# Top-32 attention, FFN and mixture of experts on one core: second-layer weights in the key and value buffers, and a third transpose buffer

## The chip, the core and the metric

The kernel runs on one core of one Trainium2 chip. The metric is the device time of one execution in microseconds (us), lower is better. A step below is one turn of the kernel's planned loop.

## What is computed

```python
# q, k, v: 4 batches x 8 heads x 576 x 64
scores = scale * np.matmul(q, k.transpose(0, 1, 3, 2))
kth = np.partition(scores, -32, axis=-1)[..., -32:-31]
scores = np.where(scores >= kth, scores, -1e9)
attn = softmax(scores)                       # written out in the reference
x = (attn @ v).transpose(0, 2, 1, 3).reshape(2304, 512)
h = np.maximum(np.maximum(x @ w1, x @ w2), x @ w3)      # 512 -> 768
x = h @ w_out                                           # 768 -> 512
logits = x @ w_gate                                     # 8 experts
expert_idx = np.argmax(logits, axis=1)
gate_w = softmax(logits)[arange, expert_idx]
for e in range(8):                                      # each token, one expert
    ye = np.maximum(x[mask_e] @ w1[e], 0.0) @ w2[e]     # 512 -> 1024 -> 512
    out[mask_e] = gate_w[mask_e, None] * ye
```

## The kernel before, in words

Every fp32 operand is kept as a sum of two fp16 parts, hi and lo, and a product is three matmuls (hi hi, hi lo, lo hi). A weight piece is split where it is loaded: ScalarE writes the hi part, scales the fp32 piece into a PSUM tile, and VectorE subtracts (`split_piece`, `lo_part`, lines L734 and L735).

**The loop of steps.** The 4 x 8 heads of 576 queries are 144 tiles of 128 queries. A Python loop plans the whole program: at step t it starts tile t (scores on TensorE, ScalarE's copy of them `s` at L890, VectorE's scan in chunks at L904) and issues for older tiles the later stages, each at a fixed lag: the candidates' rounds, threshold, k-th value, exponential (`st_exp`, L1031), mask, the probabilities' hi part `phl` (L1042, ScalarE), their lo part (L1046, GpSimd), a transposing DMA on SP's queue from `phl` to `pt` (`st_ptr`, L1051), and two steps later the matmuls of `pt` with the values (`av`, L1065). Tiles with n % 4 above 1 ("early") take the exponential in the step of the split's predecessor, `t - L_MASK`; the others at `t - L_EXP`, one step earlier, and their mask follows as VectorE's bulk work at `t - L_MASK`. There are three `phl` tiles and two `pt` buffers; TensorE must have read a `pt` before SP may issue the next transposition into it, and what SP's queue holds behind waits with it.

**Work between.** Each step also has credits with which `run_units` issues units of other work: the FFN's jobs (18 blocks of 128 tokens; six units of 36 matmuls of 128 columns at L356, two with WO, the gate, and a ranking that counts tokens per expert, L1224 and L1225), and, from the middle on, slots of the fullest expert. A slot is 128 tokens of that expert, gathered as soon as enough are ranked. Early slots run the first layer in two halves in the attention, with weights W1h, one half of the columns at a time: `half_piece` loads its four pieces of 128 x 512 in four steps through one staging tile `he` (L1300 is the split's ScalarE copy; there are three such loads, the last at steps 124 to 127); results go to a DRAM buffer `hs`. Their second layer (`unit_e2`, four units of six matmuls of 512 columns, L367 to L369) needs W2e. In the kernel before, W2e is a tile of a pool `e1` that opens at step 145, and its eight pieces load at steps 146 to 153. Each slot's `hTe` is read back from `hs` on SP's queue (L1356), two at a time.

**The end.** The last tile's av is at step 157. From there TensorE has FFN jobs, second layers, and late slots; when all blocks are ranked, `finale` goes through the other experts' tiles in the order of a table that VectorE makes from the ranking's counts (its last operation is at L332), the first of them with a transposing load (L428) on SP.

**Memory.** Keys (`kT`) and values (`vh`, `vl`) of a batch have two buffers each, taken in turn by batches 0 to 3. `hsel` keeps nine selection values per query of every group of four tiles. Ahead of step 0 the K and Q pieces are split into tiles of the pools `e` (four) and `f` (two) (`split_tile`).

The lines of the planner that set the credits and the weights' time:

```python
credit[0] = min(credit[0] + (TAIL_RATE if e2 else EARLY_RATE if slots else UNIT_RATE), 2.5 if e2 else CAP)
elif e1 and len(eld) < (KE + 2 * KD if e2 else KE):
    after(2, piece(len(eld)))
```

## Time and profile before

| | us |
|---|---|
| median of 3 runs | 979.85 |
| lowest and highest | 979.28, 984.86 |
| the profiled execution | 983.39 |
| its span | 981.7 |
| last av ends | 758.06 |
| last ranking matmul starts | 818.53 |

Busy shares of the span: TensorE (PE) 77%, VectorE (DVE) 77%, ScalarE (ACT) 71%, GpSimd (POOL) 62%. These are means over an attention in which all of them work and a tail in which TensorE does nearly alone. A row of the stretches gives, for a stretch from A to B, its length and each engine's busy time and number of instructions; PEld is TensorE's weight load. A row of waits names the waiting instruction, the engine and line that ended the wait, and the sums. In a timeline, brackets behind a row tell how long the engine was idle before it, and for what. SPq and ACTq are the queues' own times for issuing a DMA, not the transfers.

### The profile page before, as it was taken

What the parts mean: (1) busy time and instruction counts of PE and PEld (TensorE: products, weight loads), DVE (VectorE), ACT (ScalarE), POOL (GpSimd) and SP (SyncE); (2) the same over time, 40 slices, a digit from 0 to 9 for tenths busy, and PEclk for the clock granted to TensorE, in tenths of its full rate; (3) what the DMA queues carried; (4) which work ended last, traced back from release to release, by engine and by line L of the source; (5) the groups of instructions that cost most, each with busy time, mean ns of one, the idle gap of its engine ahead of it and who ended that gap; (6) DMA issues with size and microseconds to landing.
All of it is one profiled execution on the core that took longest, in us unless ns stands there. A gap on an engine that the chain in (4) does not pass through costs nothing. (4 is left out here: it accounts for less than half of the span.)

```text
span 981.7 us, 28988 instructions
## 1 busy us (share of the span) xinstructions
PE 754.9 (77%) x10606; PEld 581.5 (59%) x10606; DVE 757.6 (77%) x3109; ACT 695.2 (71%) x1462; POOL 605.9 (62%) x553
## 2 busy tenths in 40 slices
PE   0212358888887898968798896889887999999992
PEld 0100237667556586856677675677765775678781
DVE  4999999998897998978987996898934335457671
ACT  2678899998888788988978787688663231456661
POOL 1457798999696789968766888588862221111110
PEclk9999979999998999999899899899999999999997
DMA  9672987868987887999978786588668477799270
GB/s 254 177 240 58 210 154 133 139 128 126 194 151 163 127 159 139 188 172 151 181 129 135 142 143 144 107 138 142 129 137 175 127 207 263 187 295 230 56 208 16
DMA packets 372164, 155.93 MB, mean 159 GB/s; under 512 B 331931, under 2 KB 348319, under 8 KB 372000
## 3 DMA queue, kind: packets, MB, share of 16 engines
q1 hardware_dynamic: 368128, 143.10, 72.8%
q0 software_dynamic: 3136, 9.46, 3.0%
q8 instruction: 87, 1.43, 0.6%
q10 hardware_dynamic: 736, 1.32, 0.5%
q14 instruction: 77, 0.63, 0.3%
HBM read 76.06 MB, written 16.67 MB: 94 GB/s over the span
## 5 line engine op out<-in xcount | busy, mean ns | idle before, releaser
L356 PEld LDWEIGHTS <-W 128*128 128x128 f16 x4560 | 252.6, 101 | 28.3 <-issue 23.0
L956 POOL TENSOR_TENSOR f<-s,g 128x576 f32<-128x576 f32 x144 | 192.6, 1337 | 75.3 <-ACT g L950 29.0
L356 PE MATMUL mm<-xT,W 128*128 128x128 f16 x3456 | 218.4, 226 | 22.3 <-DVE W1h L735 11.7
L883 PE MATMUL S<-kT,qT 128*128 128x512 f16 (+3 forms) x640 | 109.7, 316 | 132.7 <-ACT s L890 116.3
L1046 POOL TENSOR_TENSOR phl<-e,phl 128x576 f16<-128x576 f32 x144 | 188.2, 1307 | 24.4 <-ACT phl L1042 22.1
L904 DVE MAX8 c<-s 128x8 f32<-128x96 f32 x864 | 174.7, 242 | 19.1 <-ACT s L890 18.7
L883 PEld LDWEIGHTS <-qT 128*128 128x128 f16 (+1 forms) x640 | 55.6, 107 | 192.8 <-issue 160.4
L1065 PE MATMUL av<-vh,pt 128*128 128x65 f16 (+3 forms) x1600 | 110.6, 200 | 37.1 <-DMA pt<-phl 22.1
L1042 ACT ACTIVATE phl<-e 128x576 f16<-128x576 f32 x144 | 97.6, 678 | 38.2 <-DMA pt<-phl 38.0
L1065 PEld LDWEIGHTS <-pt 128*128 128x128 f16 (+3 forms) x2400 | 88.4, 102 | 51.8 <-DMA pt<-phl 24.7
L1031 ACT ACTIVATE e<-s,be 128x576 f32<-128x576 f32 x144 | 110.4, 767 | 4.9 <-POOL s L1025 3.2
L965 DVE MAX8 vec<-f 128x8 f32<-128x576 f32 x144 | 108.8, 756 | 3.8 <-POOL f L956 1.0
L950 ACT ACTIVATE g<-s,bf 128x576 uint16<-128x576 f32 x144 | 111.0, 771 | 0.1
L890 ACT ACTIVATE s<-S 128x576 f32<-128x576 f32 x144 | 92.1, 640 | 12.8 <-PE S L883 12.0
L1036 DVE SCALAR_TENSOR_TENSOR e<-s,kth,e 128x576 f32<-128x576 f32 x72 | 100.0, 1389 | 0.0
L1065 PE MATMUL av<-vl,pt 128*128 128x64 f16 (+3 forms) x800 | 100.0, 197 | 0.0
L457 DVE SCALAR_TENSOR_TENSOR W<-st,W 128x1024 f16<-128x1024 f32 x56 | 65.8, 1221 | 38.3 <-ACT W L456 33.2
L1025 POOL TENSOR_TENSOR s<-s,g 128x576 f32<-128x576 f32 x72 | 95.2, 1322 | 0.3
L1149 POOL TENSOR_TENSOR hhl<-a,hhl 128x384 f16<-128x384 f32 x36 | 36.6, 1016 | 33.4 <-ACT hhl L1148 33.4
L356 PE MATMUL mm<-xTe,W1h 128*128 128x128 f16 x768 | 51.0, 229 | 7.5 <-DMA xTe<-xs 5.7
L456 ACT ACTIVATE W<-st 128x1024 f16<-128x1024 f32 x56 | 55.5, 1047 | 0.0
L1022 ACT ACTIVATE g<-s,kth 128x576 uint16<-128x576 f32 x72 | 55.3, 768 | 0.0
(222 smaller groups left out, 1533.1 us busy)
## 6 DMA issues: line engine op xcount, KB each, us to landing
st<-in_moe_w_dram SPq DMA_DIRECT2D x72, 512.0 KB
raw<-in_moe_w_dram SPq DMA_DIRECT2D x12, 512.0 KB
st<-in_v_dram SPq DMA_DIRECT2D x16, 256.0 KB
hs<-he SPq DMA_DIRECT2D x16, 256.0 KB
st<-in_moe_w_dram SPq DMA_DIRECT2D x16, 256.0 KB
hTe<-hs SPq DMA_DIRECT2D x8, 512.0 KB
st<-in_q_dram SPq DMA_DIRECT2D x15, 256.0 KB
qT<-qT SPq DMA_DIRECT2D x30, 128.0 KB
```

What stands on the lines that cost most here:

```text
L356: nc.tensor.matmul(out=ps[:, o * n:(o + 1) * n], lhsT=w(b, kk, c), rhs=x(a, kk), start=(kk == 0 and i == 0), stop=(kk == KD - 1 and i == 2))
L883: nc.tensor.matmul(out=ps[o:o + m, j, 0:(REM if j else NQ * P)], lhsT=qt[:, vv, hh, 0:m], rhs=kr[:, hh] if j else km[:, hh // HG, :, hh % HG],
L904: nc.vector.max(out=c[:, i * 8:(i + 1) * 8], in_=s[:, i * CW:(i + 1) * CW])
L950: nc.scalar.activation(out=gg[n], in_=Ss[n], func=ACTF.Sign, bias=bf[g][:, i], accum_out=cnt[g][:, i])
L956: nc.gpsimd.tensor_tensor(out=ff[n], in0=Ss[n], in1=gg.pop(n).bitcast(F16), op=ALU.subtract)
L965: bulk.append(lambda: nc.vector.max(out=y8[g][:, i, 1:9], in_=y))
L1025: nc.gpsimd.tensor_tensor(out=Ss[n], in0=Ss[n], in1=zz.pop(n).bitcast(F16), op=ALU.subtract)
L1031: nc.scalar.activation(out=e, in_=Ss.pop(n) if early(n) else Ss[n], func=ACTF.Exp, scale=ESC, bias=be[g][:, i])
L1036: nc.vector.scalar_tensor_tensor(out=e, in0=Ss.pop(n), scalar=kth[g][:, i:i + 1], in1=e, op0=ALU.is_ge, op1=ALU.mult)
L1042: nc.scalar.activation(out=ph[:, 0, 0:S], in_=p, func=ACTF.Copy)
L1046: nc.gpsimd.tensor_tensor(out=ph[:, 1, 0:S], in0=p, in1=ph[:, 0, 0:S], op=ALU.subtract)
L1065: nc.tensor.matmul(out=av[o:o + m, i, 0:n], lhsT=t[0:kk, p * NCH + c, o:o + m], rhs=v_rows(x, b, c, hh)[:, 0:n], start=(c == 0 and p == 0 ...
```

## The change

Keys and values of the even batches get a pool of their own, `kvl`, with one tile each (`kt0`, `vh0`, `vl0`), which batch 2 is the last to use; the odd batches have the pools of before with one buffer. When batch 2's scores are through (from step 109, pieces 0 to 3 into `kt0`) and its av are through (from step 124, pieces 4 to 7 into `vh0` and `vl0`), the W2e pieces are written there, through the three staging tiles `st` that K, Q and V used. With all eight loaded, the early slots' second layers are issued in the attention, one slot at a time until `e1` opens and two after that, and the credits of a step grow by 1.8 (`LATE_RATE`) instead of 1.4. `half_piece` uses the same staging, and its third load comes at steps 128 to 131 instead of 124 to 127. `pt` gets a third buffer. To pay for the memory: the exponential of the other half of the tiles goes to the step of its mask, with three `e` tiles instead of four (`NE3`, also in `split_tile`); `hsel` keeps two groups, and the verdict counts the k-th values above zero (`hkth`) instead of `hsel`'s ones; small tiles have fewer buffers. The gate's weights load at step 0 instead of 5, and the values' column of ones isn't written again for batch 2.

```diff
-    NSWAP, XLAG, KLAG, TSTOP, EARLY_RATE = 4, 2, 2, 140, 1.4
+    NSWAP, XLAG, KLAG, TSTOP, EARLY_RATE, LATE_RATE = 4, 2, 2, 140, 1.4, 1.8
...
+        NE3 = L_LO - L_MASK + 1
...
+            kvl = p1.enter_context(tc.tile_pool(name="kvl", bufs=1))
+            kt0 = kvl.tile([P, H * S], F16, name="kt0")
+            vh0 = kvl.tile([P, NCH, H, D + 1], F16, name="vh0")
+            vl0 = kvl.tile([P, NCH, H, D], F16, name="vl0")
...
-            kv_p = p_at.enter_context(tc.tile_pool(name="kv", bufs=2))
+            kv_p = p_at.enter_context(tc.tile_pool(name="kv", bufs=1))
...
-            k_p = p_op.enter_context(tc.tile_pool(name="kp", bufs=2))
+            k_p = p_op.enter_context(tc.tile_pool(name="kp", bufs=1))
...
-                hsel = a_p.tile([P, NG, G, 9], F16, name="hsel")
+                hsel = a_p.tile([P, NHS, G, 9], F16, name="hsel")
+                hkth = a_p.tile([P, NG, G], F32, name="hkth")
...
-                    tag = ("e", L_LO - L_EXP + 1) if lead_n[0] < L_LO - L_EXP + 1 else ("f", NFB)
+                    tag = ("e", NE3) if lead_n[0] < NE3 else ("f", NFB)
...
-                    kt = k_p.tile([P, H * S], F16, tag="kT", name="kT")
+                    kt = k_p.tile([P, H * S], F16, tag="kT", name="kT") if b % 2 else kt0
...
-                e = wk_p.tile([P, S], F32, tag="e", name="e", bufs=L_LO - L_EXP + 1)
+                e = wk_p.tile([P, S], F32, tag="e", name="e", bufs=NE3)
...
-                t = wk_p.tile([P, 2 * NCH, P], F16, tag="pt", name="pt", bufs=L_AV - L_PTR)
+                t = wk_p.tile([P, 2 * NCH, P], F16, tag="pt", name="pt", bufs=L_AV - L_PTR + 1)
...
+            FREE = 3 * (NTL // B)
+
+            def w2e(e, kk):
+
+                if kk < KE // 2:
+                    return kt0[:, (e * (KE // 2) + kk) * DM:(e * (KE // 2) + kk + 1) * DM]
+                y = (vh0, vl0)[e].rearrange("p t h d -> p (t h d)")
+                return y[:, (kk - KE // 2) * DM:(kk - KE // 2 + 1) * DM]
+
+            def stage():
+                return e1[0].tile([P, DM], F32, tag="st", name="st", bufs=3) if e1 else stage_tile()
+
+            def piece_ok(i):
+
+                if i >= KE:
+                    return bool(e2) and i < KE + 2 * KD
+                return bool(picked) and clock[0] > picked + 8 and clock[0] > FREE + (0 if i < KE // 2 else L_AV + 1)
...
-                st = ew[0].tile([P, DM], F32, tag="he", name="he")
+                st = stage()
...
-                            if sum(o.hT is not None and not o.late and o.u < 8 for o in slots) < 2:
-                                s.hT = e1[0].tile([P, 2 * KE, P], F16, tag="hTe", name="hTe", bufs=2)
+                            if sum(o.hT is not None and not o.late and o.u < 8 for o in slots) < (2 if e1 else 1):
+                                s.hT = (e1 or ew)[0].tile([P, 2 * KE, P], F16, tag="hTe", name="hTe",
+                                                          bufs=2 if e1 else 1)
...
-                credit[0] = min(credit[0] + (TAIL_RATE if e2 else EARLY_RATE if slots else UNIT_RATE), 2.5 if e2 else CAP)
+                credit[0] = min(credit[0] + (TAIL_RATE if e2 else LATE_RATE if len(eld) >= KE else EARLY_RATE if slots
+                                             else UNIT_RATE), 2.5 if e2 else CAP)
...
-                    n = t - L_EXP
+                    n = t - L_MASK
                     if ok(n) and not early(n):
                         st_exp(n)
...
-                    elif e1 and len(eld) < (KE + 2 * KD if e2 else KE):
-                        after(2, piece(len(eld)))
+                    elif piece_ok(len(eld)):
+                        (after(2, piece(len(eld))) if e1 else pend_w.append(piece(len(eld))))
                         eld.append(t)
```

The order of ScalarE shows the pieces and the exponential. Here are about two steps of before, around step 125: L890 is the score copy of a new tile, L950 and L1022 are older tiles' selections, L1042 writes `phl`, L1300 and L734 split a piece of W1h.

```order
L1022 ACTIVATE g<-s,kth 128x576
L1042 ACTIVATE phl_143<-e 128x576
L1300 ACTIVATE W1h<-he 128x512
L734 ACTIVATE mm<-he 128x512
L940 ACTIVATE bf<-T_12353 128x1
L890 ACTIVATE s<-S 128x576
L950 ACTIVATE g,cnt<-s,bf 128x576
L1022 ACTIVATE g<-s,kth 128x576
L1042 ACTIVATE phl_144<-e 128x576
L1300 ACTIVATE W1h<-he 128x512
L734 ACTIVATE mm<-he 128x512
```

The same two steps after the change (the lines are some 10 to 30 higher; L1328 is the ScalarE copy of a piece, L1043 the exponential):

```order
L1034 ACTIVATE g<-s,hkth 128x576
L1054 ACTIVATE phl_149<-e 128x576
L1328 ACTIVATE vh_108<-st 128x512
L740 ACTIVATE mm<-st 128x512
L1043 ACTIVATE e<-s,be 128x576
L949 ACTIVATE bf<-T_12381 128x1
L899 ACTIVATE s<-S 128x576
L959 ACTIVATE g,cnt<-s,bf 128x576
L1034 ACTIVATE g<-s,hkth 128x576
L1054 ACTIVATE phl_150<-e 128x576
L1328 ACTIVATE vh_108<-st 128x512
L740 ACTIVATE mm<-st 128x512
```

Where a piece of W1h was split, one of W2e is now, into `vh0`; W1h's pieces follow four steps later. An exponential stands between the piece and the next score copy.

The order of SP ahead of the finale's first tile, before (L449 loads weights of the next expert, L1356 the last slot's `hTe`, L428 the first tile's rows):

```order
L449 ISA
L449 DMA st_15743<-in_moe_w_dram 128x2x512
L449 ISA
L449 DMA st_15743<-in_moe_w_dram 128x2x512
L1356 DMA hTe<-hs 128x2048
L422 TENSOR_LOAD roi
L422 ISA x2
L428 ISA
L428 DMA_TRANSPOSE W1h<-xs 128x8x128
L429 ISA
L429 DMA mt<-xs 128x2
```

And after (L448, L427):

```order
L448 ISA
L448 DMA st_15821<-in_moe_w_dram 128x2x512
L448 ISA
L448 DMA st_15821<-in_moe_w_dram 128x2x512
L421 TENSOR_LOAD roi
L421 ISA x2
L427 ISA
L427 DMA_TRANSPOSE W1h<-xs 128x8x128
L428 ISA
L428 DMA mt<-xs 128x2
```

The load of `hTe` no longer stands between the weights and the first tile's rows.

The order of TensorE behind the last ranking (L1225 before, L1237 after) differs in what stands ahead of it. Before:

```order
L368 LDWEIGHTS hTe
L368 MATMUL mm<-W2e,hTe 128x512
L369 LDWEIGHTS hTe
L369 MATMUL mm<-W2e,hTe 128x512
L1224 LDWEIGHTS tri_70
L1224 MATMUL mm<-oh,tri_70 128x8
L1225 LDWEIGHTS ones_69
L1225 MATMUL mm<-oh,ones_69 128x8
L367 LDWEIGHTS hTe
L367 MATMUL mm<-W2e,hTe 128x512
```

After (`W1e` belongs to a late slot's first layer, `kt` is the tile that now holds half of W2e):

```order
L355 LDWEIGHTS W1e
L355 MATMUL mm<-xTe,W1e 128x128
L355 LDWEIGHTS W1e
L355 MATMUL mm<-xTe,W1e 128x128
L1236 LDWEIGHTS tri_70
L1236 MATMUL mm<-oh,tri_70 128x8
L1237 LDWEIGHTS ones_69
L1237 MATMUL mm<-oh,ones_69 128x8
L366 LDWEIGHTS hTe
L366 MATMUL mm<-kt_107,hTe 128x512
```

A unit of a second layer stood ahead of the last ranking; now a late slot's first layer stands there, since eight units of second layers are issued further ahead. Second layers follow the ranking in both.

## Rows read from the trace of the kernel before

**Rows 1.** Stretches: us, busy us (x instructions) by engine, PEclk, DMA share, GB/s.

```profile
140.20:236.10 95.90, 79.25 (x1176) 62.24 (x1174) 90.81 (x440) 89.12 (x201) 90.48 (x75) 0.94 0.76 137
578.60:643.70 65.10, 52.74 (x850) 42.39 (x847) 50.44 (x234) 49.35 (x112) 47.81 (x41) 0.90 0.72 131
643.70:689.90 46.20, 41.62 (x620) 33.20 (x618) 41.82 (x216) 39.21 (x92) 39.56 (x36) 1.00 0.88 148
689.90:758.00 68.10, 51.90 (x786) 43.51 (x783) 38.01 (x102) 37.69 (x75) 38.73 (x36) 0.92 0.68 135
758.00:849.60 91.60, 91.60 (x873) 58.76 (x872) 41.24 (x152) 27.87 (x49) 18.11 (x26) 1.00 0.69 192
849.60:955.00 105.40, 105.18 (x1747) 85.82 (x1746) 64.33 (x71) 62.45 (x79) 14.56 (x14) 1.00 0.79 208
```

**Rows 2.** Timeline of PE behind the attention: start us, us, engine, line, operation.

```profile
758.06 8.21 PE L356 MATMUL mm<-xT,W 128*128 128x128 f16 x144
...
766.41 0.38 PE L367 MATMUL mm<-W2e,hTe 128*128 128x512 f16 x1
...
772.67 0.38 PE L369 MATMUL mm<-W2e,hTe 128*128 128x512 f16 x1
...
818.53 0.17 PE L1225 MATMUL mm<-oh,ones 128*128 128x8 f16 x1
```

**Rows 3.** Waits of SP's own queue, whole span: us in total, times, longest us.

```profile
SPq L1051 <- PE av L1065: 130.0, 53, 5.9
```

**Rows 4.** Tile pt, who waited for it: us in total, times.

```profile
  ACT phl L1042: 38.0, 32
```

**Rows 5.** Waits of DVE from 24 to 690 us.

```profile
DVE W1h L735 <- ACT mm L734: 26.6, 8, 7.5
DVE c L904 <- ACT s L890: 18.7, 18, 2.3
```

**Rows 6.** Groups by shape: xcount, busy us, mean ns, idle us before them.

```profile
L1031 ACT ACTIVATE e<-s,be 128x576 f32<-128x576 f32 x144 | 110.4, 767 | 4.9 <-POOL s L1025 3.2 <-POOL phl L1046 1.5
...
L735 DVE TENSOR_TENSOR W1h<-mm,W1h 128x512 f16<-128x512 f32 x11 | 7.6, 688 | 26.6 <-ACT mm L734 26.6
L1300 ACT ACTIVATE W1h<-he 128x512 f16<-128x512 f32 x12 | 7.5, 627 | 9.8 <-DMA he<-in_moe_w_dram 9.7
```

**Rows 7.** Timeline of ACT, four steps in which pieces of W1h are split.

```profile
604.79 0.63 ACT L890 ACTIVATE s<-S 128x576 f32<-128x576 f32 x1
...
611.70 0.63 ACT L1300 ACTIVATE W1h<-he 128x512 f16<-128x512 f32 x1 [2.36 <-DMA he<-in_moe_w_dram]
...
625.70 0.63 ACT L1300 ACTIVATE W1h<-he 128x512 f16<-128x512 f32 x1 [1.72 <-DMA he<-in_moe_w_dram]
...
632.72 0.63 ACT L890 ACTIVATE s<-S 128x576 f32<-128x576 f32 x1
```

**Rows 8.** Waits of PE from 689.9 to 758 us.

```profile
PE av L1065 <- DMA pt<-phl: 9.7, 6, 2.7
PE mm L356 <- DVE W2e L735: 2.9, 1, 2.9
```

**Rows 9.** Timelines of DVE and SP behind the last ranking.

```profile
831.03 0.18 DVE L332 TENSOR_TENSOR chg<-new,live 1x31 int32<-1x31 f32 x1
...
838.17 0.34 SPq L1356 DMA_DIRECT2D hTe<-hs  x1
839.26 1.29 SPq L428 DMA_TRANSPOSE W1h<-xs  x1
```

**Rows 10.** Timelines of SP and ACT in the lead-in.

```profile
5.37 2.00 SPq L787 DMA_TRANSPOSE qT<-e  x1
...
8.80 2.62 SPq L773 DMA_TRANSPOSE kT<-e  x2
...
15.34 1.84 SPq L773 DMA_TRANSPOSE kT<-f  x1
...
10.13 1.30 ACTq L791 DMA_DIRECT2D qT<-qT  x2
```

More of the change, by code (lines that the diff above doesn't have):

```diff
@@ L156, in late_consts @@
         def late_consts():
-            nc.sync.dma_start(out=wg32, in_=w_gate.rearrange("(k p) e -> p k e", p=P))
             nc.scalar.activation(out=wg[:, 0], in_=wg32, func=ACTF.Copy, scale=SC)
@@ L366, in second_layer @@
                 hi, lo = h[:, hilo(0, kk), :], h[:, hilo(1, kk), :]
-                nc.tensor.matmul(out=ps, lhsT=hi, rhs=w[:, 0, kk, :], start=(kk == 0), stop=False)
-                nc.tensor.matmul(out=ps, lhsT=hi, rhs=w[:, 1, kk, :], start=False, stop=False)
-                nc.tensor.matmul(out=ps, lhsT=lo, rhs=w[:, 0, kk, :], start=False, stop=(kk == KE - 1))
+                nc.tensor.matmul(out=ps, lhsT=hi, rhs=w(0, kk), start=(kk == 0), stop=False)
+                nc.tensor.matmul(out=ps, lhsT=hi, rhs=w(1, kk), start=False, stop=False)
+                nc.tensor.matmul(out=ps, lhsT=lo, rhs=w(0, kk), start=False, stop=(kk == KE - 1))
         def first_half(ps, x, w):
@@ L550, in weights @@
                 listed, i = seq[n]
-                return (at("W1", i), W2[0]) if listed else (W1e, W2e)
+                return (at("W1", i), w2) if listed else (W1e, W2e)
             for n in range(NS + 1):
@@ L596, in body @@
                     if t > NMIX:
-                        stage2(n - 1, W2[0], part)
+                        stage2(n - 1, w2, part)
                     split_w2(t, 2 * part)
@@ L898, in st_chunks @@
                 s = Ss[n]
-                c = sm_p.tile([P, CAND * 8], F32, tag="c", name="c")
+                c = sm_p.tile([P, CAND * 8], F32, tag="c", name="c", bufs=2)
                 cands[n] = c
@@ L977, in st_kth @@
             def st_kth(g):
-                kt = sm_p.tile([P, G], F32, tag="kth", name="kth")
+                kt = sm_p.tile([P, G], F32, tag="kth", name="kth") if general else hkth[:, g]
                 kth[g] = kt
@@ L983, in search @@
                     def search(i):
+                        wfall = wk_p.tile([P, S], F32, tag="f", name="f", bufs=NFB)
                         src = Ss[g * G + i]
@@ L997, in st_verdict @@
             def st_verdict():
+                hit = a_p.tile([P, NG * G], F16, name="hit")
                 chain([
-                    lambda: nc.vector.tensor_reduce(out=bad[:, 0:1], in_=hsel.rearrange("p n g e -> p (n g e)"),
-                                                    axis=AX.X, op=ALU.add),
+                    lambda: nc.vector.tensor_scalar(out=hit, in0=hkth.rearrange("p n g -> p (n g)"), scalar1=0.0,
+                                                    scalar2=None, op0=ALU.is_gt),
+                    lambda: nc.vector.tensor_reduce(out=bad[:, 0:1], in_=hit, axis=AX.X, op=ALU.add),
                     lambda: nc.vector.tensor_reduce(out=bad[:, 1:2], in_=heq.rearrange("p n g e -> p (n g e)"),
@@ L1229, in post @@
                     posted[0] += 1
-                    si = sm_p.tile([P, 1], I32, tag="si", name="si")
+                    si = sm_p.tile([P, 1], I32, tag="si", name="si", bufs=2)
                     def slot():
@@ L1264, in attempt @@
             ranked, picked, counted, posted = [], 0, [0], [0]
-            slots, task, W1h, W1e, W2e, eld, hld = [], [], [], [], [], [], []
+            slots, task, W1h, W1e, eld, hld = [], [], [], [], [], []
             ew, e1, e2, half = [], [], [], [None]
@@ L1280, in piece @@
                     src = ew2[bass.ds(re, 1), i * P:(i + 1) * P, :]
-                    hi, lo = (W2e[0][:, e, i] for e in range(2))
+                    hi, lo = (w2e(e, i) for e in range(2))
                 else:
@@ L1413, in unit_e2 @@
                 ps = s.ps
-                second_layer(ps, s.hT, W2e[0], range(part * KE // 4, (part + 1) * KE // 4))
+                second_layer(ps, s.hT, w2e, range(part * KE // 4, (part + 1) * KE // 4))
                 def post():
-                    put_y(ps, mte[:, s.i], e1[0].tile([P, DM], F32, tag="ye", name="ye", bufs=2))
+                    put_y(ps, mte[:, s.i], e1[0].tile([P, DM], F32, tag="ye", name="ye", bufs=2) if e1 else stage())
                     freed()
@@ L1557, in attempt @@
                     clock[0] = t
+                    if t == 0:
+                        nc.sync.dma_start(out=wg32, in_=w_gate.rearrange("(k p) e -> p k e", p=P))
                     if t == 5:
@@ L1683, in attempt @@
                         raw.append(raw_p.tile([P, KE, DM], F32, name="st2"))
-                        second = finale(p1, ps_m, e2[0], raw, p_wt, W1h[0], W1e[0], W2e[0], ranked, lambda: len(slots),
+                        second = finale(p1, ps_m, e2[0], raw, p_wt, W1h[0], W1e[0], w2e, ranked, lambda: len(slots),
                                         lambda: all(s.open for s in slots),
```

57 lines of the change are left out of this document (29 added, 28 removed).

## The prediction

> **What bounds the kernel now.** I read the stretches first, then the waits, then single places of the timelines.
>
> The stretches show two different kernels [rows 1]. Up to 758 us several engines share the work in steps, one tile of the attention each, and none is full. Steps 24 to 48 (the first line) take 95.9 / 24 = 4.0 us; VectorE, ScalarE and GpSimd are each above 60 of 95.9 us there. Steps 120 to 131 (the second line) take 65.1 / 12 = 5.4 us, with every engine less busy than before, so they wait. Steps 132 to 142 take 46.2 / 11 = 4.2 us. From 758 us TensorE is busy 91.6 of 91.6 and 105.18 of 105.40 us: what is taken away from TensorE there comes off the end. The timeline shows its unit prices [rows 2]: the 512-column matmuls of a second layer start at 766.41 for the first and 772.67 for the thirtieth, so 6.26 / 29 = 0.216 us each and 6 x 0.216 = 1.29 us for a unit of six; 144 matmuls of the FFN's first layer take 8.21 us, 2.05 us for a unit of 36.
>
> Then the waits of the attention. SP's queue stands 130.0 us in 53 waits at its transposition of the probabilities, because TensorE still reads one of the two transpose buffers [rows 3]. ScalarE waits 38.0 us for such a transposition to have read the `phl` that it is to write next [rows 4]. VectorE, which scans the scores first, waits 18.7 us for ScalarE's copy of them [rows 5]. I read these as one chain: a late `pt` makes a late `phl`, a late ScalarE, a late VectorE, a late step. The other entry of VectorE, 26.6 us in 8 waits, is the split of W1h pieces, whose ScalarE half waits 9.7 us for the load of `he` [rows 5, 6].
>
> **The change part by part.** The sum is made against the profiled execution, 983.4 us (span 981.7), which lies 3.5 above the median of the runs shown; the difference is then set on the median, 979.85.
>
> *Tail, after the last av.* By then the new order has issued 8 more units of the early slots' second layers and 2 more first-layer units of job 14. TensorE has no gap there, so 8 x 1.29 + 2 x 2.05 = 14.4 us of work leave the tail. What is late next: behind the last ranking only 16 units remain before the finale's first tile, 16 x 1.29 = 20.7 us, and that tile's rows come by a transposing load that needs the ranking's table. Before, the last ranking matmul is at 818.53, the table's last operation on VectorE at 831.03, and the load starts at 839.26, just behind an `hTe` load at 838.17 that no longer stands there [rows 2, 9]. Without it the load starts 839.26 - 1.09 - 818.53 = 19.6 us after the ranking and lands 4.8 us later (a transposition issued at 5.37 let its first user, a copy queue, issue at 10.13 [rows 10]), at 24.4. TensorE would stand 24.4 - 20.7 = 3.7, say 3.8 us. Net -10.6; bounds -14.4 (no gap) and -5 (a gap of 9).
>
> *The last part of the attention, 690 to 758.* Of those 14.4 us of work, 8.6 are now done here and 5.8 in steps 122 to 142. TensorE is idle 68.1 - 51.9 = 16.2 us here, 12.6 of which are waits for `pt` and for a W2e piece being split [rows 1, 8]; both causes go with the third buffer and the earlier pieces. 8.6 - 12.6 = -4.0; bounds +8.6 (nothing saved) and -7.6 (all the idle time used, 8.6 - 16.2).
>
> *Second layers in steps 122 to 142.* 5.8 us of work beside (65.1 - 52.74) + (46.2 - 41.62) = 17 us idle [rows 1]. It is hidden except where it delays the scores: +1.5; bounds 0 and +5.8.
>
> *Eight W2e pieces inside the attention.* Each is a load, a copy of 0.63 us and a scaling of the same shape on ScalarE, and a subtraction of 0.69 us on VectorE [rows 6], in a step of its own. The like of it stands in the trace: four pieces of W1h in four steps, from one score copy at 604.79 to the fourth after it at 632.72 [rows 7], 27.93 us or 6.98 each, against the 4.2 of the neighbours [rows 1]. The excess is 2.8 us a piece, of which about 1.2 is the wait for the single `he` buffer (2.36 and 1.72 before two of the four). The new pieces are staged in three buffers, so 1.6: 8 x 1.6 = +12.8. Bounds: 8 x 1.0 = 8 (half of the instructions' own 0.63 + 0.63 + 0.69, as if they were half hidden) and 8 x 2.8 = 22.4. I take 12.8, from the nearest rows.
>
> *The single staging buffer of W1h.* Its pieces now use the same three buffers; the 9.8 us of waits [rows 6] go, and some of it is made up by other engines anyway: -6; bounds 0 and -9.8.
>
> *Third transpose buffer.* SP's queue no longer stops for TensorE, or a tile later; `phl` is read earlier. What VectorE can win directly is its 18.7 us [rows 5]; I take half of it, 9, because ScalarE's lateness has other causes too, and 2 for the K and Q transpositions that stand behind the waiting one in SP's queue: -11. Bounds: 0 (the wait moves on to `phl` or TensorE) and -27.7 (VectorE's 18.7, and 9, half of what ScalarE's 38.0 [rows 4] has beyond them).
>
> *The exponential one step later, with three buffers.* For half of the tiles (72) ScalarE's exponential now stands in the step of the mask that needs it, not a step before. It can cost from nothing to 72 x 0.767 = 55 us if the mask on VectorE always waits for it whole. The nearest row is the exponential itself: over all 144, also those that have run in the mask's step until now, ScalarE waits 4.9 us before it [rows 6]. I take +3. VectorE has other work of the step between, and that cover would have to be gone for more.
>
> *Lead-in.* A split fewer has a buffer of its own, so the last one waits for the K transposition of the fourth, second of a pair that starts at 8.80 and takes 2.62 [rows 10]: issued at 10.1, landed at 14.9, split at 15.5, its own transposition at about 16.7 instead of 15.34. Between 0 and +1.4, as long as the first scores hang on it; +0.5.
>
> Sum: -10.6 - 4.0 + 1.5 + 12.8 - 6 - 11 + 3 + 0.5 = -13.8. On the median: **966.0 us**. The attention as a whole gains 3.2, the tail 10.6.
>
> One rule of the Trainium skill speaks against the first term ("Perfetto Trace Analysis", § Identifying the Most-Contended Engine): the busy percentage of matmuls is no measure of TensorE, that of weight loads is. In 758 to 849.6 the weight loads are busy 58.76 of 91.6 us, 64% [rows 1]. By that rule the tail would not be full and only 64% of 14.4 would come off, 9.2, or 5.4 net of the gap. Against it stand the starts of the matmuls, one every 0.216 us without a hole [rows 2]; I give it a small chance below.
>
> **The rivals.**
> *The third buffer gains nothing.* The 130 us of SP [rows 3] are a queue's, not an engine's: TensorE's av comes when it comes, and the wait of SP goes to `phl` or to the probabilities. For it: SP's 130 stand against only 18.7 on VectorE. Against it: ScalarE's 38.0 [rows 4], and TensorE's own 9.7 us for `pt` [rows 8]. Then -13.8 + 11 = -2.8: 977.
>
> *The third buffer frees the pace.* All of 27.7 is won. For it: no engine is full up to 758 us. Against it: GpSimd, at 89.12 of 95.90 us in the first stretch [rows 1], and ScalarE would be the next bounds. -13.8 - 16.7: 949.
>
> *The pieces cost more than all the rest (the slower side).* Eight steps each take a piece whose subtraction stands in VectorE's queue behind ScalarE; the longest such wait is 7.5 us [rows 5]. If a piece costs the middle of 7.5 and 2.8, 5.2 us, eight cost 41 instead of 12.8: -13.8 + 28.4 = +14.6, 994. It decides from 12.8 + 13.8 = 26.6, 3.3 us a piece. For it: ScalarE is at 90.81 of 95.90 us in a full stretch and at 50.44 of 65.1 where W1h pieces run, so it is late without being full. Against it: 9.7 of the 26.6 us stand behind loads into `he`, and the pieces now have three buffers.
>
> *The tail isn't full*, by the rule above: 966 + 5.2 = 971.
>
> **How the numbers follow.** Forecast 0.47, third buffer nothing 0.22, third buffer everything 0.18, pieces 0.08, tail not full 0.05. About 1% (9.8 us: 970.05 and 989.65) is what a measurement of this kernel can tell from no change. Faster by more: two thirds of the forecast's 0.47, all of 0.18, and 0.06 of the others, 0.56. Slower by more: most of the pieces' 0.08, 0.06. Within 1%: 0.38. The range must leave out 0.2 at most: the pieces' case above, and about half of the case in which the third buffer gives all below; 944 to 986. That also takes in the forecast with the pieces at 2.8 us each (976) and the exponential at several times my value.
>
> **What would show it.** In the changed profile: TensorE's stretch from the last av to the end about 10 us shorter, with a gap of some 4 us behind the last second layer and before the finale's first tile; SP's wait for av much below 130.0, and ScalarE's wait for `pt` below 38.0; VectorE's wait for the score copy near 10 instead of 18.7; no waits for `he`; steps 109 to 112 and 124 to 127 about 1.6 us longer each than their neighbours; the mask waiting little for the exponential. The forecast is wrong if the steps of the pieces take 7 us or more, if the last av ends later than before by more than its own added work, if the mask on VectorE shows tens of microseconds of waiting for the exponential, or if the gap behind the last ranking is above 9 us.

## The result and the profile after

| | us |
|---|---|
| before, median of 6 runs | 981.03 (979.28 to 984.86) |
| changed, median of 6 runs | 952.21 (950.46 to 958.18) |
| ratio, 95% interval | 0.9708, 0.9675 to 0.9742 |
| profiled execution of the changed kernel, its span | 951.46, 949.7 |
| forecast | 966.0, range 944 to 986 |

The change saved 28.8 us, twice the 13.8 that were forecast. The sign was right, the time lies in the range, and the tail came near its forecast; the attention gave more than it was said to.

The stretches of the changed kernel, cut at the same events as the lines of [rows 1]: the score copies of steps 108, 132 and 143, the end of the last av, and TensorE's last matmul (us, then busy us and instructions of PE, PEld, DVE, ACT, POOL, then PEclk, DMA share, GB/s).

```profile
517.04:630.53 113.49, 100.75 (x1587) 83.00 (x1587) 99.41 (x467) 98.58 (x223) 93.82 (x80) 0.92 0.79 154
630.53:681.63 51.10, 48.18 (x647) 36.00 (x645) 44.70 (x225) 41.66 (x96) 42.29 (x38) 0.97 0.82 161
681.63:739.81 58.18, 56.23 (x897) 47.02 (x895) 29.99 (x93) 31.34 (x63) 39.51 (x38) 1.00 0.83 147
739.81:932.69 192.88, 190.68 (x2598) 141.45 (x2598) 108.78 (x225) 92.23 (x129) 29.66 (x37) 1.00 0.67 191
```

Before, the same four take 118.79, 46.2, 68.2 and 206.1 us (524.88 to 643.67, to 689.89, to 758.1, to 964.24); the second and third are in [rows 1], the first and the last are:

```profile
524.88:643.67 118.79, 101.44 (x1601) 83.37 (x1601) 102.18 (x462) 92.81 (x210) 92.25 (x80) 0.91 0.74 131
758.10:964.24 206.14, 205.86 (x2719) 150.30 (x2718) 110.68 (x228) 94.04 (x132) 33.84 (x41) 1.00 0.71 192
```

The first is 5.3 shorter although six pieces more are split in it (all eight of W2e and two of W1h, where there were four of W1h), the second 4.9 longer, the third 10.0 shorter, the tail 13.3 shorter. From 681.63 to 739.81 TensorE is now busy 56.23 of 58.18 us; in the last part before it was busy 51.90 of 68.10 [rows 1]. The last part of the attention has hardly any holes left.

SP's own queue (us in total, times, longest us), answering to [rows 3]; then who waited for a `pt`, answering to [rows 4]; VectorE's waits from 24 to 690 us, answering to [rows 5]; and groups by shape, answering to [rows 6], the first of them (L1036) that of the mask before.

```profile
SPq L1063 <- PE av L1077: 54.5, 27, 5.3
SPq L1063 <- POOL phl L1058: 35.4, 30, 3.0
SPq L1063 <- POOL f L965: 34.7, 28, 4.0
```

```profile
  ACT phl L1054: 11.3, 10
```

```profile
DVE W1h L741 <- ACT mm L740: 10.7, 8, 2.8
...
DVE c L913 <- ACT s L899: 4.7, 8, 1.5
...
DVE e L1048 <- ACT e L1043: 2.9, 3, 1.8
```

```profile
L1036 DVE SCALAR_TENSOR_TENSOR e<-s,kth,e 128x576 f32<-128x576 f32 x72 | 100.0, 1389 | 0.0
...
L1048 DVE SCALAR_TENSOR_TENSOR e<-s,hkth,e 128x576 f32<-128x576 f32 x72 | 104.1, 1446 | 8.3 <-ACT e L1043 8.1
...
L1328 ACT ACTIVATE W1h<-st 128x512 f16<-128x512 f32 x12 | 7.5, 624 | 2.9 <-DMA st<-in_moe_w_dram 2.9
```

SP's wait for TensorE falls from 130.0 to 54.5 us, ScalarE's for the transposition from 38.0 to 11.3, VectorE's for the score copy from 18.7 to 4.7, and ScalarE's wait for a piece of W1h to be loaded from 9.7 to 2.9. The mask on VectorE (L1048) now waits 8.1 us for the exponential, 2.9 of them up to 690 us, where it waited for nothing.

The timelines of the changed kernel behind the last ranking and in the lead-in (TensorE, VectorE, SP), answering to [rows 2, 9, 10]:

```profile
796.36 0.17 PE L1237 MATMUL mm<-oh,ones 128*128 128x8 f16 x1
...
819.33 2.84 PE L355 MATMUL ph<-W1h,W1e 128*128 128x128 f16 x48 [2.06 <-DMA W1h<-xs]
...
809.27 0.18 DVE L331 TENSOR_TENSOR chg<-new,live 1x31 int32<-1x31 f32 x1
...
816.14 1.30 SPq L427 DMA_TRANSPOSE W1h<-xs  x1
...
16.65 1.24 SPq L779 DMA_TRANSPOSE kt<-f  x1
```

The finale's first tile waits 2.06 us for its rows; 3.8 was forecast. Their load starts 816.14 - 796.36 = 19.8 us after the ranking (19.6 forecast). In the lead-in the last transposition of K is issued at 16.65 (16.7 forecast), and the first score copy still starts at 22.9, against 23.3 before: it costs nothing.

### The profile page after: what moved, and what is told of

Same layout as the page of the kernel before. It is cut to its first block, busy times and chain, and to the rows that moved or that the text cites. A ratio compares the mean times of both kernels' runs of the same rounds, so it can differ in the third digit from the quotient of the medians.

```text
span 949.7 us, 29065 instructions
## 1 busy us (share of the span) xinstructions
PE 751.6 (79%) x10606; PEld 578.1 (61%) x10606; DVE 762.5 (80%) x3110; ACT 694.3 (73%) x1463; POOL 608.6 (64%) x552
## 5 line engine op out<-in xcount | busy, mean ns | idle before, releaser
L355 PEld LDWEIGHTS <-W 128*128 128x128 f16 x4560 | 248.2, 100 | 28.0 <-issue 25.2
L965 POOL TENSOR_TENSOR f<-s,g 128x576 f32<-128x576 f32 x144 | 200.9, 1395 | 69.6 <-DVE vec L974 32.9
L355 PE MATMUL mm<-xT,W 128*128 128x128 f16 x3456 | 210.5, 222 | 18.2 <-DVE W1h L741 6.8
L1058 POOL TENSOR_TENSOR phl<-e,phl 128x576 f16<-128x576 f32 x144 | 186.3, 1293 | 8.1 <-ACT phl L1054 7.9
L892 PE MATMUL S<-kt,qT 128*128 128x64 f16 (+3 forms) x320 | 62.4, 345 | 109.9 <-ACT s L899 94.4
L1043 ACT ACTIVATE e<-s,be 128x576 f32<-128x576 f32 x144 | 110.6, 768 | 7.7 <-POOL phl L1058 5.7
L1048 DVE SCALAR_TENSOR_TENSOR e<-s,hkth,e 128x576 f32<-128x576 f32 x72 | 104.1, 1446 | 8.3 <-ACT e L1043 8.1
L1077 PEld LDWEIGHTS <-pt 128*128 128x128 f16 (+3 forms) x2400 | 90.8, 104 | 30.5 <-issue 17.6
L1054 ACT ACTIVATE phl<-e 128x576 f16<-128x576 f32 x144 | 97.4, 676 | 11.3 <-DMA pt<-phl 11.3
L899 ACT ACTIVATE s<-S 128x576 f32<-128x576 f32 x144 | 92.3, 641 | 15.5 <-PE S L892 14.6
L892 PE MATMUL S<-kT,qT 128*128 128x512 f16 (+3 forms) x320 | 48.5, 293 | 18.7 <-ACT s L899 18.7
L1034 ACT ACTIVATE g<-s,hkth 128x576 uint16<-128x576 f32 x72 | 55.4, 769 | 0.0
L1161 POOL TENSOR_TENSOR hhl<-a,hhl 128x384 f16<-128x384 f32 x36 | 34.7, 964 | 28.9 <-ACT hhl L1160 28.9
```

What stands on the lines that cost most here:

```text
L355: nc.tensor.matmul(out=ps[:, o * n:(o + 1) * n], lhsT=w(b, kk, c), rhs=x(a, kk), start=(kk == 0 and i == 0), stop=(kk == KD - 1 and i == 2))
L892: nc.tensor.matmul(out=ps[o:o + m, j, 0:(REM if j else NQ * P)], lhsT=qt[:, vv, hh, 0:m], rhs=kr[:, hh] if j else km[:, hh // HG, :, hh % HG],
L965: nc.gpsimd.tensor_tensor(out=ff[n], in0=Ss[n], in1=gg.pop(n).bitcast(F16), op=ALU.subtract)
L1043: nc.scalar.activation(out=e, in_=Ss.pop(n) if early(n) else Ss[n], func=ACTF.Exp, scale=ESC, bias=be[g][:, i])
L1048: nc.vector.scalar_tensor_tensor(out=e, in0=Ss.pop(n), scalar=kth[g][:, i:i + 1], in1=e, op0=ALU.is_ge, op1=ALU.mult)
L1054: nc.scalar.activation(out=ph[:, 0, 0:S], in_=p, func=ACTF.Copy)
```

## The experiments

Ratios are to the kernel before on the same chip, with 95% intervals. A per cent is 9.8 us. "pt2" and the like are names of runs; after2 is the changed kernel again. Three parts are told apart: the third transpose buffer, the late exponential, and the move of W2e's pieces with the second layers behind them.

| run | what it is | ratio | interval |
|---|---|---|---|
| changed | all of it, first measurement | 0.9708 | 0.9675 to 0.9742 |
| after2 | all of it, beside best1b, shift and hold | 0.970 | 0.9662 to 0.9738 |
| pt2 | two transpose buffers | 0.991 | 0.9875 to 0.9945 |
| pt2_exp8 | two, and the exponential early | 0.9843 | 0.9799 to 0.9887 |
| nomove | W2e after the attention | 0.9787 | 0.9751 to 0.9824 |
| nomove_exp8 | the same, exponential early | 0.9712 | 0.9675 to 0.9749 |
| hold | pieces moved, second layers not | 0.9761 | 0.9737 to 0.9785 |
| twice | eight pieces more | 0.9851 | 0.9819 to 0.9884 |
| shift | pieces four steps later | 0.9781 | 0.9755 to 0.9807 |
| best1 | exponential early, two staging buffers | 0.968 | 0.963 to 0.973 |
| best1b | the same again | 0.969 | 0.9658 to 0.9723 |
| b_stage | before, W1h staged in three buffers | 1.001 | 0.9981 to 1.0039 |

**Two transpose buffers (pt2).**

```diff
-                t = wk_p.tile([P, 2 * NCH, P], F16, tag="pt", name="pt", bufs=L_AV - L_PTR + 1)
+                t = wk_p.tile([P, 2 * NCH, P], F16, tag="pt", name="pt", bufs=L_AV - L_PTR)
```

> The changed kernel with two transpose buffers instead of three, all else as changed. Theory A (the third buffer carries the gain): some 16 to 20 us slower than the changed kernel, 968 to 972, with SP's wait for av back above 100 us and ScalarE's wait for the transposition near 38. Theory B (it gave the forecast 11 or less): 957 to 963.

Ratio 0.991: without the third buffer 2% of the 3% are gone, some 20 us. Its waits of SP, of ScalarE for `pt`, and the mask's group:

```profile
SPq L1063 <- PE av L1077: 146.5, 60, 7.4
```

```profile
  ACT phl L1054: 33.0, 24
```

```profile
L1048 DVE SCALAR_TENSOR_TENSOR e<-s,hkth,e 128x576 f32<-128x576 f32 x72 | 106.4, 1478 | 18.5 <-ACT e L1043 18.3
```

SP waits 146.5 us again and ScalarE 33.0, as theory A had it. ScalarE's 33.0 are 21.7 more than in the changed kernel, about the size of the loss, but not at its place: 16.9 of them lie behind 690 us, while the score copy of step 108 is already 15.5 us later than in the changed kernel (532.57 against 517.04), with ScalarE's wait only 7.2 longer (9.8 against 2.6 from 24 to 525 us). Of the mask's 18.3 us of waiting for the exponential, 6.0 lie ahead of the last score copy (703.86) and 12.3 behind it.

**The exponential early, with two transpose buffers (pt2_exp8).**

```diff
-                    n = t - L_MASK
+                    n = t - L_EXP
                     if ok(n) and not early(n):
                         st_exp(n)
...
-        NE3 = L_LO - L_MASK + 1
+        NE3 = L_LO - L_EXP + 1
```

(and `pt` as in pt2, which pays for the fourth `e`)

> As pt2, and the exponential back a step earlier with four buffers of its own: against pt2 this is the price of the late exponential alone. Forecast: 3 us faster than pt2. Rival: the late exponential costs nothing, since VectorE waits for it 8.1 us in all and has slack elsewhere; then the same within 1 us, or slower by a few us because ScalarE's order ahead of the score copy was better with the late one.

Ratio 0.9843 against pt2's 0.991: the late exponential costs 0.7%, 6.6 us, twice the forecast, when there are two transpose buffers. The mask's group:

```profile
L1048 DVE SCALAR_TENSOR_TENSOR e<-s,hkth,e 128x576 f32<-128x576 f32 x72 | 95.7, 1329 | 4.3 <-ACT e L1043 4.3
```

Its wait falls from 18.3 to 4.3 us, and a mask takes 1329 ns instead of 1478. What counts of the wait is the part up to 690 us, 6.0 before and nothing here: the two profiles are 7.5 us apart at step 108 (532.57 and 525.09), and behind the last score copy, where most of the wait stood, they differ by 0.7.

**No move (nomove).**

```diff
-                return bool(picked) and clock[0] > picked + 8 and clock[0] > FREE + (0 if i < KE // 2 else L_AV + 1)
+                return bool(e1)
...
-    NSWAP, XLAG, KLAG, TSTOP, EARLY_RATE, LATE_RATE = 4, 2, 2, 140, 1.4, 1.8
+    NSWAP, XLAG, KLAG, TSTOP, EARLY_RATE, LATE_RATE = 4, 2, 2, 140, 1.4, 1.4
```

> The changed kernel without the move: W2e's pieces load after the attention again, second layers run there, the credit rate stays 1.4; third transpose buffer, late exponential and three-buffer staging stay. Theory A (the third buffer gave more than the 11 us forecast, and a W2e piece costs about the 1.6 us forecast): the last score copy starts some 13 us earlier than in the changed kernel, near 669 us, and the time is about 952 + 16 - 13 = 955. Theory B (the pieces cost little, under 0.5 us each): the last score copy stays near 680, and the time is about 952 + 16 = 968, 16 being the tail's 14.4 and a bit of the wait for the split of a W2e piece that comes back.

Ratio 0.9787, 7.8 us above the changed kernel, between theory A's 3 and theory B's 16. Its stretches, cut as those of the changed kernel:

```profile
517.98:635.16 117.18, 99.01 (x1584) 81.61 (x1584) 106.48 (x459) 92.79 (x212) 91.36 (x80) 0.94 0.75 137
635.16:679.49 44.33, 43.90 (x649) 35.75 (x647) 43.19 (x219) 39.23 (x93) 39.49 (x36) 0.97 0.72 140
679.49:739.69 60.20, 50.54 (x776) 42.58 (x774) 37.37 (x104) 37.49 (x77) 38.48 (x36) 0.91 0.81 166
739.69:944.51 204.82, 204.82 (x2718) 150.00 (x2718) 110.14 (x228) 93.97 (x132) 33.88 (x41) 1.00 0.69 189
```

The last score copy starts at 679.49, not near 669: on the whole the eight pieces and the second layers beside them make the attention up to there 2.1 us longer, not 14. The third stretch is already 60.20 us, so 8.0 of the 10.0 us saved there come without the move. They don't need the third buffer either: in pt2, which has the move and two buffers, the last av ends 61.47 us after the last score copy (765.33 and 703.86). Either part brings most of it. The tail is 204.82 against 192.88 (195.8 in after2): that part is the move's, 9 to 12 us.

**The pieces alone (hold).** Pieces as in the changed kernel, second layers as before.

```diff
-                if len(eld) >= KE and eld[KE - 1] + 2 < clock[0]:
+                if e1 and len(eld) >= KE and eld[KE - 1] + 2 < clock[0]:
```

(and `LATE_RATE` 1.4)

> The changed kernel with W2e's pieces loaded in the attention, but the second layers held back until step 145 and the credit rate left at 1.4. It tells the pieces from the second layers. If the second layers cost the 1.5 us forecast in steps 122 to 142, the last score copy starts 1 to 2 us earlier than in the changed kernel. If they cost what steps 132 to 142 show (51.1 us against 44.3 without the move), it starts 5 to 7 us earlier. The time: 5 to 8 us above the changed kernel, as most of the tail's gain goes.

Ratio 0.9761. Between nomove and hold (0.26%, 2.6 us faster, the intervals overlap) lies the moving of eight pieces: it costs nothing that can be measured. Between hold and the changed kernel lie the second layers and the credit rate: 0.6%, 6 us, as expected.

```profile
518.18:642.04 123.86, 100.14 (x1564) 81.78 (x1564) 105.76 (x478) 99.42 (x223) 95.97 (x83) 0.90 0.72 140
642.04:689.03 46.99, 43.91 (x656) 34.87 (x653) 42.36 (x202) 40.46 (x94) 37.86 (x32) 1.00 0.77 136
689.03:746.98 57.95, 52.85 (x810) 44.96 (x807) 29.14 (x102) 29.64 (x60) 38.55 (x36) 0.94 0.84 149
```

The last score copy starts at 689.03, 7 to 9 us later than in the changed kernel (681.63 in its first trace, 679.9 in after2), where both expectations had it earlier. The profiled execution, span 965.9, lies some 5 us above this run's median of 962.32, and its excess is in steps 108 to 131 (123.86 us), where up to step 127 its order is that of the changed kernel. The mean granted clock of TensorE in these steps was 0.90 here, 0.92 in the changed kernel and 0.98 in after2 (110.00 us); whether it made the steps long or long steps brought it down, no run tells. So a stretch of a single execution is good to some 5 us, no better. Two readings hang less on that, as the profiles agree on them. The second stretch is 46.99 here, and 51.10 (51.86 in after2) with 24 matmuls of second layers in it, 5.2 us of work at 0.216 [rows 2]. The third is 57.95 with 12 such matmuls and 58.18 with 24, where the further ones cost nothing.

**Eight pieces more (twice).**

```diff
+                    elif 113 <= t <= 120:
+                        pend_w.append(piece((t - 113) % 4))
                     elif len(hld) < KD and half[0] is not None:
```

> The changed kernel with eight pieces more: in steps 113 to 120, which had none, pieces 0 to 3 of W2e are loaded and split again, twice, with the same values into the same place. It measures a piece by itself. Prediction's price, 1.6 us each: 12.8 us slower than the changed kernel, the score copies of steps 108 to 124 spread over 12 us more. Rival: what made the four W1h steps long was the FFN's and ranking's work in them, and a piece costs 0.3 to 0.6 us, as the run without the move says (2.1 us in all for eight pieces and the second layers beside them): 2 to 5 us slower.

Ratio 0.9851 against 0.970 to 0.9708: 14 us for eight, 1.75 each (1.2 to 2.4 by the intervals). The prediction's price was 1.6. ScalarE's score copies of steps 108 and 124 in this run, the same two in the changed kernel, and the added pieces' groups from 539 to 579 us:

```profile
518.58 0.63 ACT L899 ACTIVATE s<-S 128x576 f32<-128x576 f32 x1
...
601.39 0.64 ACT L899 ACTIVATE s<-S 128x576 f32<-128x576 f32 x1
```

```profile
517.04 0.63 ACT L899 ACTIVATE s<-S 128x576 f32<-128x576 f32 x1
...
588.03 0.64 ACT L899 ACTIVATE s<-S 128x576 f32<-128x576 f32 x1
```

```profile
L741 DVE TENSOR_TENSOR kt<-mm,kt 128x512 f16<-128x512 f32 x8 | 5.5, 692 | 8.8 <-ACT mm L740 8.8
...
L740 ACT ACTIVATE mm<-st 128x512 f32<-128x512 f32 x8 | 4.7, 590 | 0.1
...
L1328 ACT ACTIVATE kt<-st 128x512 f16<-128x512 f32 x7 | 4.4, 624 | 0.2 <-DMA st<-in_moe_w_dram 0.2
```

82.8 us against 71.0 (68.5 in after2), 11.8 more. A piece has 0.62 + 0.59 + 0.69 = 1.9 us of instructions, and little of them is hidden in these steps.

**Four steps later (shift).**

```diff
-... clock[0] > FREE + (0 if i < KE // 2 else L_AV + 1)
+... clock[0] > FREE + (4 if i < KE // 2 else L_AV + 5)
```

> The changed kernel with W2e's pieces four steps later (113 to 116, 128 to 131), so that W1h's third load keeps its old steps 124 to 127. If a piece costs what the doubled pieces showed, 1.75 us, and the eight were cheap because the masks on VectorE got shorter (16.1 us in steps 108 to 131 against 26.9 without the move), then steps 108 to 131 less their masks take 95 to 100 us here too, and the time goes up by what the masks take above 16. If a piece were cheap by itself, those steps less their masks take about 91, as without the move.

Ratio 0.9781: 0.8% slower than the changed kernel, by position, to which belongs that the second layers start four steps later too (12 instead of 24 of their matmuls in steps 132 to 142).

```profile
518.91:640.12 121.21, 100.32 (x1564) 83.42 (x1564) 104.31 (x477) 98.89 (x223) 94.68 (x83) 0.90 0.73 145
640.12:691.02 50.90, 48.63 (x694) 37.87 (x691) 41.63 (x215) 41.64 (x95) 37.68 (x32) 0.97 0.91 156
```

Steps 108 to 131 take 121.2 us, 7.7 more than in the changed kernel. The masks in them take 18.4 us (16.1 in the changed kernel), so they explain 2.3 of it; less the masks there are 102.8 us, outside the 95 to 100 of the one theory and the 91 of the other. But in hold, where the pieces stand as in the changed kernel, the same steps less their masks take 103.9 us (123.86 less 19.96), so this stretch alone doesn't tell position from chance; the medians on one chip do, 964.84 against after2's 953.92. Why the later place is dearer stays open.

**Staging (b_stage, nomove_he).** The kernel before with W1h's pieces in the three staging buffers, and the changed kernel without the move with the single one:

```diff
-                st = ew[0].tile([P, DM], F32, tag="he", name="he")
+                st = stage_tile()
```

```diff
-                st = stage()
+                st = ew[0].tile([P, DM], F32, tag="he", name="he")
```

> The kernel before with one edit: the pieces of W1h are staged in the three buffers of K, Q and V instead of the single one. Forecast of the prediction: 6 us faster than before, 974 against 980, the 9.8 us wait for the load gone. Rival: the pieces then wait in SP's queue behind a transposition that waits for TensorE, and nothing is gained, 980.

> The changed kernel without the move, and with the single staging buffer for W1h's pieces again. If the single buffer made the 9.8 us of waits before ScalarE's copy of a piece, they are back near 9 us here. If they came from SP's queue, where the load stood behind a transposition that waited for TensorE, they stay near the 2.6 us of the run without the move, since that queue waits little with three transpose buffers.

b_stage: 1.001, nothing. nomove_he, a single run: 965.73 us. ScalarE's copy of a piece, first in b_stage, then in nomove_he, and SP's wait in the latter; last, the copy of a piece in pt2:

```profile
L1300 ACT ACTIVATE W1h<-st 128x512 f16<-128x512 f32 x12 | 7.5, 626 | 10.0 <-DMA st<-in_moe_w_dram 10.0
```

```profile
L1328 ACT ACTIVATE W1h<-he 128x512 f16<-128x512 f32 x12 | 7.5, 626 | 2.6 <-DMA he<-in_moe_w_dram 2.4
```

```profile
SPq L1063 <- PE av L1077: 43.6, 23, 4.8
```

```profile
L1328 ACT ACTIVATE W1h<-st 128x512 f16<-128x512 f32 x12 | 7.5, 622 | 3.1 <-DMA st<-in_moe_w_dram 3.1
```

Three staging buffers and a queue that waits for TensorE: 10.0 us. One buffer and a queue that waits little (43.6 us): 2.4. nomove itself, with three, has 2.6. So the number of staging buffers changes nothing, on either side. That the load of `he` waited for SP's queue, behind a transposition that waits for TensorE, fits these two runs but not pt2: there the queue waits 146.5 us for TensorE, and the copies of W1h's pieces only 3.1 for their loads. In the first two of the three loads, whose steps are the same in all these runs, they wait 4.9 us before, 5.8 in b_stage, 3.1 in pt2 and 1.7 in the changed kernel. The third `pt` buffer may have a part in it; what the rest hung on stays open.

**The third buffer almost alone (nomove_exp8).** nomove, with the exponential early in four buffers, as in pt2_exp8.

> The changed kernel without the move, and with the exponential back a step earlier in four buffers: of the change's parts only the third transpose buffer, the staging and the smaller tiles are left. If the late exponential costs the 6 to 8 us that two transpose buffers showed, this is 957 to 959 on the scale of the run without the move's 964. Rival: with the third buffer the late exponential is hidden, since the mask's wait fell from 18.3 to 3.1 us: 963 to 965.

Ratio 0.9712, 0.75% below nomove, as by the 6 to 8 us that two transpose buffers showed; but its last score copy starts at 679.53 in the profiled execution, and nomove's at 679.49. The ratios say that the late exponential costs 7 us with three buffers too, the traces say that it costs nothing up to there. The profiled execution here was the longest of its six, 966.37 us against a median of 961.19, so the trace may show this kernel slower than it mostly is; the question stays open.

**Both better parts (best1, best1b).** The changed kernel, exponential early in four buffers, paid for by `ST` 2 instead of 3.

> The changed kernel with the exponential back a step earlier in four buffers, paid for by two staging buffers instead of three. If staging buffers are worth nothing (as the kernel before with three of them for W1h showed) and the late exponential costs 6 us, ratio to before 0.964 to 0.966. If the late exponential is hidden by the third transpose buffer, or two staging buffers make the pieces wait for loads, 0.970 to 0.975.

> The changed kernel with the exponential a step earlier in four buffers and two staging buffers, again, beside the changed kernel. If the late exponential costs 6 us with three transpose buffers too, 0.6% faster than the changed kernel, the score copies of steps 108 to 143 up to 3 us earlier; if three transpose buffers hide it, the two are the same within 0.3%.

> The changed kernel itself, beside the three others of this call on one chip. Ratio to before 0.968 to 0.974, as measured.

0.968 and 0.969, beside 0.9708 and 0.970 of the changed kernel; beside each other on one chip, 954.46 against 953.92 us. The first lies between its two expectations, and the two kernels are the same within what was measured. Either the late exponential is hidden here, or the two staging buffers take what it gives; which, is open.

**Steps 24 to 143 in six of the runs.** One line each, from the score copy of step 24 to that of step 143: before, nomove_exp8, nomove, pt2_exp8, pt2, changed.

```profile
140.16:689.89 549.73, 461.04 (x6867) 368.66 (x6865) 485.54 (x2337) 465.52 (x1047) 451.86 (x385) 0.94 0.84 148
139.05:679.53 540.48, 464.92 (x6871) 370.29 (x6869) 501.35 (x2334) 463.43 (x1046) 448.21 (x384) 0.93 0.79 150
139.59:679.49 539.90, 461.58 (x6883) 369.92 (x6881) 505.43 (x2336) 464.67 (x1047) 452.14 (x384) 0.93 0.81 150
139.79:695.72 555.93, 466.45 (x6883) 372.18 (x6881) 494.62 (x2345) 473.25 (x1063) 453.25 (x386) 0.94 0.81 151
139.59:703.86 564.27, 469.46 (x6883) 373.00 (x6881) 508.44 (x2349) 473.97 (x1063) 456.01 (x386) 0.93 0.81 149
139.01:681.63 542.62, 468.07 (x6883) 370.17 (x6881) 501.29 (x2350) 472.86 (x1062) 457.57 (x386) 0.94 0.81 156
```

Without the move, the third buffer shortens these steps by 9.3 us (nomove_exp8) or, with the late exponential, 9.8 (nomove). With two buffers, the move lengthens them by 6.2 (pt2_exp8) and the late exponential by 8.3 more (pt2). With three, the late exponential costs nothing here and the move 2.7. So of the 21.7 us between pt2 and the changed kernel some 9 are the buffer's own; the rest is what it hides of the other two parts. Each line is one execution, good to some 5 us, but the medians don't add up either: 15 us for pt2_exp8 and 28 for nomove_exp8, against 28.8 for the whole change. The smaller tiles were in no run by themselves; up to step 108 they do nothing, as pt2_exp8 reaches its score copy at 525.09 us and before at 524.88.

## Why the prediction was right or wrong

The time fell within the range, but the gain was twice the forecast, and several terms missed. By place, against the profiles: up to the last score copy +0.8 forecast and -8.3 measured, the last part of the attention -4.0 and -10.0, the tail -10.6 and -13.3.

*The third buffer.* Its -11 was meant for the steps up to the last score copy, and there it was about right: third buffer, staging and late exponential together were forecast at -14, and nomove, which has just these and the smaller tiles, is 9.8 shorter; with nothing for staging (b_stage) and nothing for the late exponential (nomove against nomove_exp8), -11 stands against -9.8. As a whole the buffer is worth more: 20 us when it is taken out of the changed kernel (pt2), and nomove_exp8, where it is almost the only change, is 28 below before by its median (17 by its profile); the upper bound was 27.7. The step took the parts one by one, and missed that with two buffers the late exponential and the move cost 8.3 and 6.2 us in steps 24 to 143, and that 8 us come behind the last score copy. Which row of before would have given the size, the runs don't show: of ScalarE's wait 38.0 [rows 4] nomove loses 30.9 and gains 21 us, and VectorE's wait for the score copy falls by 15.7 (18.7 to 3.0) for 9.8 in these steps. (The bound took half of 38.0 - 18.7 as 9; it is 9.65.) The rival "the third buffer frees the pace", 949, had the time right but not the reason: the pace of steps 24 to 48 hasn't risen, 98.59 us now and 95.90 before [rows 1].

```profile
139.01:237.60 98.59, 82.33 (x1195) 64.25 (x1193) 96.21 (x441) 88.81 (x202) 89.78 (x75) 0.98 0.70 136
```

There the prediction had also read the columns one place off: 90.81 us (and 50.44 in steps 120 to 131) are VectorE's, 89.12 are ScalarE's and GpSimd has 90.48. Three engines are busy 93 to 95% in steps 24 to 48, which "none is full" understates. No term of the sum rests on it.

*The single staging buffer was no cause.* The forecast credited -6 to it. b_stage shows 0, with 10.0 us of the same waits in three buffers, and nomove_he shows 2.4 with one. What the 9.8 us hung on stays open: they are as small in pt2 (3.1), where SP's queue waits for TensorE as long as before.

*The eight pieces are the term that missed most.* 1.6 us forecast for a piece, and 1.75 measured in steps that had none (twice). But +12.8 for the eight was wrong: hold against nomove is -2.6 us, and pieces and second layers together make steps 24 to 143 only 2.7 us longer (nomove to changed), where +14.3 was forecast. The pieces weren't added but moved, and what they cost at their old place comes back, some 2 us (the last part takes 60.20 in nomove, 57.95 in hold); the prediction had counted 2.9 us of TensorE's wait for them [rows 8] there. The 11.6 us that are missing in steps 24 to 143 have no shown cause. The masks in steps 108 to 131 take 10.8 us less in the changed kernel than in nomove, which would cover most of them, but no run tells why they do. The slow rival, 994, needed 3.3 us a piece and fell.

*Second layers in steps 122 to 142.* +1.5 forecast. Steps 132 to 142 took 46.99 in hold and 51.10 in the changed kernel: about 4 us for 5.2 us of work, inside the bound of 5.8, but hardly hidden.

*The last part of the attention.* -4.0 forecast, -10.0 measured, beyond the bound of -7.6. Of that, 8.0 are there without the move (nomove, 60.20) and 6.7 without the third buffer (pt2, 61.47), so one cause of the idle time was enough to remove. The step added 8.6 us of second layers to these steps; there were 24 such matmuls, 5.2 us at 0.216. TensorE is busy 5.7 us longer than in nomove (56.23 against 50.54), and the stretch is 2 us shorter all the same: the added work went into idle time.

*The tail.* -10.6 forecast; 13.3 shorter in the profile, 10.3 in after2's (gaps of 2.06 and 3.16 us, 3.8 forecast). TensorE was full there, as the starts of the matmuls said [rows 2]. The Trainium skill ("Perfetto Trace Analysis", § Identifying the Most-Contended Engine) names two measures for TensorE, the share of the peak FLOP rate and the busy share of weight loads. By the second alone, as the prediction worked it out, 5.4 would have come off; the traces don't agree with that. The first wasn't worked out.

*The late exponential.* +3 forecast, 6.6 with two transpose buffers, 0 to 7 with three. The other work of VectorE that was to cover it covers it better with the third buffer: up to 690 us the mask waits 2.9 us in the changed kernel and 6.0 in pt2.

Luck had a part: the -6 for staging and the +12.8 for the pieces, both wrong, stood against each other in the sum. The lead-in's transposition was right to 0.05 us and cost nothing.

## What to carry to other kernels

A buffer that a queue waits for is not worth one fixed sum: it also hides what other parts of a change cost, so parts that are priced one by one need a run with each of them left out. A wait for a load into a single buffer does not show that a second buffer would help (b_stage). When work is moved, look up what it costs at its old place before it is counted as added. And a piece of work that costs 1.75 us in one step can cost almost nothing in others: where a step has room is found by moving it.

## What the runs showed that was not expected

A mask on VectorE takes from 0.8 to 7.1 us, with operands of the same shape. The timelines of VectorE and GpSimd in nomove, two masks and GpSimd's operations around the second:

```profile
624.13 0.81 DVE L1048 SCALAR_TENSOR_TENSOR e<-s,hkth,e 128x576 f32<-128x576 f32 x1
...
627.83 4.86 DVE L1048 SCALAR_TENSOR_TENSOR e<-s,hkth,e 128x576 f32<-128x576 f32 x1
...
627.10 1.28 POOL L1058 TENSOR_TENSOR phl<-e,phl 128x576 f16<-128x576 f32 x1
628.34 1.27 POOL L1037 TENSOR_TENSOR s<-s,g 128x576 f32<-128x576 f32 x1
629.58 1.26 POOL L965 TENSOR_TENSOR f<-s,g 128x576 f32<-128x576 f32 x1
630.81 1.26 POOL L1058 TENSOR_TENSOR phl<-e,phl 128x576 f16<-128x576 f32 x1
```

The mask at 624.13 takes 0.81 us. The one at 627.83 takes 4.86 and ends at 632.69, just behind the last of four GpSimd operations that follow one another from 627.10 to 632.07 with no gap. The masks of steps 108 to 131 take 22.2 us before, 26.9 without the move, 16.1 in the changed kernel, 13.3 in after2 and 20.0 in hold. The Trainium skill ("SBUF — State Buffer", § Who interferes with whom) says that a VectorE instruction with two inputs in SBUF contends with a GpSimd instruction that reads SBUF. This trace agrees, with 4.86 us against 0.81. It may be part of why the same pieces cost differently in different steps; the runs don't settle it. It also takes back some of what the third buffer gives: from before to nomove, VectorE's busy time in steps 24 to 143 grows from 485.54 to 505.43 us, while all the masks together grow from 100.0 to 116.9 us. VectorE's idle time there falls by 30 us, and only 9.8 come off these steps.
